# Fourteen attention pairs with both halves of the product with V in one step, on a fused attention and feed-forward kernel

## The chip, the cores and the metric

One NeuronCore of a Trainium2 chip runs the whole program. The metric is the device time of one execution in microseconds (us); the profiled execution is one more run, taken with the hardware profiler.

## The reference

Causal attention with a decay per position, then two feed-forward layers on its output:

```python
scores = scale * np.matmul(q, k.transpose(0, 1, 3, 2))      # (4, 8, 576, 576), head size 64
cum = np.cumsum(np.log(np.clip(f, 0.0001, 1.0)), axis=-1)
decay = cum[:, :, :, None] - cum[:, :, None, :]
scores = np.where(causal, -1000000000.0, scores + decay)
scores = scores - np.max(scores, axis=-1, keepdims=True)
attn = np.exp(scores)
attn = attn / (np.sum(attn, axis=-1, keepdims=True) + 1e-09)
x = np.matmul(attn, v)                                      # then (2304, 512)
h = x @ w_in;  y = (h * np.clip(h + 3.0, 0.0, 6.0) / 6.0) @ w_out
h = y @ w_in2; out = (np.maximum(h, 0.0) + alpha * np.minimum(h, 0.0)) @ w_out2
```

## The kernel before

The 32 heads are taken as 16 pairs (p = 0 to 15). A pair is nine units, and the attention loop makes one step for each unit: four of the first head (128 queries each, positions 0 to 3 of the pair), one joint unit for the last 64 queries of both heads (position 4), four of the second head (positions 5 to 8). A unit goes through the loop as a pipeline. At its own step TensorE makes its scores (`stage1`, L406 to L408, or L418 to L422 for the joint one); one step later VectorE takes the row maxima (`maxes`, L382); two steps later ScalarE takes the exponentials (`exps`, L389); five steps later TensorE transposes them (L437) and VectorE or ScalarE copies them out of PSUM (`evac`, L448, for the joint unit L452 and L455). The table `EV` says which engine copies: VectorE for the units with i = 3 (positions 3 and 8, 128x512), ScalarE for all others.

The scores lie in four PSUM banks that are used in turn. A unit takes the next bank, the joint one the next two, so a pair takes ten, and the scores at position n of a pair (0 to 3) go into the bank that position 5 + n of the pair before used. They wait until ScalarE has read it (`reader`).

The order within a step is written out by hand: transposes, maxima, exponentials, evacuations, work put down in `todo`, scores, and last the side work of `side`. Each engine takes its instructions in that order. The lists `CONV_ATT`, `CONV_ATT1` and `BUILD_ATT` give side work with its step: the unpacking of weights (m on ScalarE, L141; f and s on VectorE, L144 and L148; j, the join, L152; g, the sign, L157), their split into high and low parts (L195 on ScalarE, L199 on GpSimd), and the split of the attention output (L259 on ScalarE, L264 on GpSimd).

The product with V of pair p (`stage3`) falls into the steps of pair p + 1. It has two parts: queries 0 to 255 (part 0) and 256 to 575 (part 1). VectorE multiplies each part's result by the reciprocal sums (L502). In pairs 0, 1, 3 and 5 (`PIECE`) both parts are issued at position 7 of the next pair, part 0 into a PSUM buffer of the transposes (`pw`). In the other pairs part 0 is issued at position 6 and part 1 at position 8, and both use the one buffer `pv`, which the joint unit's `tq` (L441, position 0 of the pair after) uses too.

For the next heads, GpSimd scales and copies the query and the key (`prep_head`, L96) at positions 3 (`QA`) and 7 (`QB`) of each pair, GpSimd makes the key's low part (`low_k`, L370) and VectorE the query's (`low_q`, L375). The `low_q` of the head prepared at position 7 runs two steps later, at position 0 of the next pair, and the other at position 6.

After the attention the two feed-forward layers run on TensorE almost without a gap. At the very end `piece7` adds up partial products; for the text "23" it puts three operations at the front of the current step's list.

## Time and profile before

| | |
|---|---|
| median of 3 runs | 955.18 us (955.0 to 955.51) |
| the profiled execution's own time | 956.1 us |
| its span, first to last instruction | 953.9 us |
| mean granted TensorE clock | 0.998 |
| TensorE busy | 943.2 us, 99% |
| VectorE, ScalarE, GpSimd busy | 728.3, 552.6, 682.3 us |
| the chain that ended last | TensorE 91% of the span |

The time of an execution is a little longer than its span: 2.2 us lie around the span here. Busy TensorE time contains short waits inside of a run of matmuls, so the 99% don't say that nothing can be gained. The attention takes about the first 200 us, and there the start of one and the same instruction of each pair (the mask matmul of the joint unit, L422) shows how long a pair took.

### The profile page before, as it was taken

Reading aid. Unit: us, or ns where it says so; the run is one execution under the profiler, and the core shown is the slowest. Engines: PE = TensorE matmul, PEld = TensorE weight load, DVE = VectorE, ACT = ScalarE, POOL = GpSimd, SP = SyncE. Lnnn points to the kernel's source line nnn. Section 1 sums busy time; section 2 is a strip of 40 time slices with the busy share of each in tenths; the row PEclk is TensorE's granted clock in tenths of the full one; section 3 lists DMA queues with packets and bytes.
Section 4 is the critical chain, followed back from the end, with each engine's and each line's share of the span. In section 5 each row is a group of like instructions: output and inputs, shape, how many; then the busy total and the mean of one; then the engine's idle time right before and its main releaser. Section 6 shows DMA issues by size and latency. Waiting matters only on the chain.

```text
span 953.9 us, 16501 instructions
## 1 busy us (share of the span) xinstructions
PE 943.2 (99%) x5710; PEld 864.5 (91%) x5710; DVE 728.3 (76%) x1283; ACT 552.6 (58%) x1357; POOL 682.3 (72%) x670
## 2 busy tenths in 40 slices
PE   8999999999999999999999999999999999999998
PEld 5777777798999999999999999989899899899997
DVE  7899999857687877786788565357798778758787
ACT  6888887856654555464745366644445545464551
POOL 8678998666766466685766199666765678598886
PEclk9999999999999999999999999999999999999999
DMA  6766777301444344211587732414634420565641
GB/s 209 236 196 200 221 245 217 108 23 49 152 182 154 116 188 182 73 45 34 193 322 261 295 135 76 154 66 173 228 103 181 188 89 12 189 233 196 266 185 69
DMA packets 39511, 153.71 MB, mean 161 GB/s; under 512 B 5228, under 2 KB 5228, under 8 KB 36324
## 3 DMA queue, kind: packets, MB, share of 16 engines
q1 hardware_dynamic: 39424, 152.65, 45.2%
q8 instruction: 45, 0.74, 0.3%
q14 instruction: 38, 0.31, 0.1%
q10 hardware_dynamic: 4, 0.00, 0.0%
HBM read 101.40 MB, written 47.09 MB: 156 GB/s over the span
## 4 chain that ended last, share of the span: by engine, by line
PE 91%; DVE 4%; POOL 2%; ACT 1%; issue 1%; DMA 1%; POOLq 0%; DVEq 0%; ACTq 0%; SPq 0%
PE hA L812 20%; PE o L850 20%; PE o L852 15%; PE hC L812 10%; PE o L927 5%; PE hB L812 5%; PE tp L437 4%; PE pv L495 3%; PE sc L406 2%; PE sc L407 2%; PE sc L418 1%; PE sc L420 1%; PE sc L408 1%; PE tr L475 1%; POOL xl L264 1%
## 5 line engine op out<-in xcount | busy, mean ns | idle before, releaser
L758 POOL TENSOR_TENSOR g<-t,g 128x384 fp32r<-128x384 f32 x164 | 178.0, 1086 | 171.5 <-ACT g L757 164.8
L850 PE MATMUL o<-g,wo 128*128 128x384 f32 x1152 | 230.9, 339 | 1.2 <-POOL g L758 1.1
L812 PE MATMUL hA<-xh,wi 128*128 128x384 f32 x768 | 225.1, 337 | 0.6 <-ACT p L389 0.3
L850 PEld LDWEIGHTS o<-g,wo 128*128 128x128 f32 x1152 | 204.1, 188 | 2.4 <-POOL g L758 2.0
L757 ACT CAST g<-t 128x384 fp32r<-128x384 f32 x164 | 84.4, 514 | 145.9 <-DVE t L749 77.6
L852 PE MATMUL o<-wo,g 128*128 128x512 f32 x612 | 158.1, 394 | 0.0
L812 PEld LDWEIGHTS hA<-xh,wi 128*128 128x128 f32 x768 | 141.6, 188 | 3.3 <-DVE hD L826 0.6
L852 PEld LDWEIGHTS o<-wo,g 128*128 128x128 f32 x612 | 113.7, 188 | 18.7 <-POOL g L758 0.5
L812 PE MATMUL hA<-xl,wi 128*128 128x384 f32 x384 | 129.5, 337 | 0.0
L859 DVE SCALAR_TENSOR_TENSOR r<-o,r 128x384 f32<-128x384 f32 x168 | 92.3, 553 | 47.2 <-PE o L850 46.6
L812 PE MATMUL hC<-xh,wi 128*128 128x384 f32 x384 | 114.0, 337 | 0.0
L870 DVE TENSOR_TENSOR r<-o,r 128x512 f32<-128x512 f32 x90 | 61.6, 686 | 40.9 <-PE o L852 40.4
L389 ACT ACTIVATE p<-sc,nm 128x128 f32<-128x128 f32 (+2 forms) x144 | 80.3, 561 | 19.2 <-DVE nm L382 15.1
L382 DVE TENSOR_REDUCE nm<-sc 128x1 f32<-128x128 f32 (+2 forms) x144 | 71.6, 508 | 13.4 <-PE sc L408 8.3
L812 PEld LDWEIGHTS hA<-xl,wi 128*128 128x128 f32 x384 | 72.1, 188 | 2.3
L812 PEld LDWEIGHTS hC<-xh,wi 128*128 128x128 f32 x384 | 70.9, 188 | 1.5 <-issue 0.2
L264 POOL TENSOR_TENSOR xl<-r,xh 128x384 fp32r<-128x384 f32 x59 | 68.9, 1180 | 2.1 <-ACT xh L259 1.5
L437 PE MATMUL tp<-ident,p 128*128 128x128 f32 x384 | 66.7, 276 | 0.3 <-ACT pt L452 0.3
L817 ACT COPY s<-hA 128x384 f32<-128x384 f32 x96 | 45.9, 478 | 34.8 <-PE hA L812 34.4
L812 PE MATMUL hC<-xl,wi 128*128 128x384 f32 x192 | 64.8, 337 | 0.0
L812 PE MATMUL hB<-xh,wi 128*128 128x384 f32 x192 | 57.0, 338 | 0.0
L406 PE MATMUL sc<-k,q 128*128 128x256 f32 (+2 forms) x128 | 54.2, 424 | 0.9 <-DVE k L370 0.8
(209 smaller groups left out, 2056.7 us busy)
## 6 DMA issues: line engine op xcount, KB each, us to landing
wid<-wi SPq DMA_DIRECT2D x24, 896.0 KB
wi<-wid SPq DMA_DIRECT2D x12, 1792.0 KB
rqk<-in_qk SPq DMA_DIRECT2D x32, 608.0 KB
raw<-in_wi SPq DMA_DIRECT2D x32, 512.0 KB
raw<-in_wo SPq DMA_DIRECT2D x32, 512.0 KB
wod<-wo SPq DMA_DIRECT2D x24, 512.0 KB
wo<-wod SPq DMA_DIRECT2D x12, 1024.0 KB
vt<-in_v SPq DMA_DIRECT2D x16, 320.0 KB
```

The lines of the kernel that those rows point to most:

```text
L264: e.tensor_sub(out=XS[k][1][:, b, c], in0=x, in1=XS[k][0][:, b, c].bitcast(F32))
L382: last = waits("V", nc.vector.tensor_reduce(out=nm, in_=src, axis=AX.X if n == 1 else AX.XY, op=ALU.max, negate=True), last)
L389: last = waits("A", nc.scalar.activation(out=o, in_=src, func=AF.Exp, bias=nm, scale=1.0, accum_out=dst), last)
L406: waits("T", nc.tensor.matmul(out=sc[:, 0:n], lhsT=q1[:, qs], rhs=k1[:, 0:n], start=True, stop=False), *free)
L437: nc.tensor.transpose(tp[:, j, :], pt[:, 128 * j:128 * j + 128], ident)
L757: nc.scalar.copy(out=gt[n][i][:, 0], in_=hold["g"])
L758: nc.gpsimd.tensor_sub(out=gt[n][i][:, 1], in0=hold["g"], in1=gt[n][i][:, 0].bitcast(F32))
L812: nc.tensor.matmul(out=h, lhsT=a, rhs=b[:, x, kc], start=new and kc + e == 0, stop=kc == KH - 1 and e == 2, skip_group_check=not new)
L850: nc.tensor.matmul(out=o[:, 0:NB], lhsT=a[:, cs], rhs=b, start=st, stop=sp)
L852: nc.tensor.matmul(out=o, lhsT=b[:, cs], rhs=a, start=st, stop=sp)
L859: later(0, lambda: nc.vector.scalar_tensor_tensor(out=acc, in0=o[:, 0:NB], scalar=1.0 / 6.0, in1=acc, op0=ALU.mult, op1=ALU.add))
L870: nc.vector.tensor_add(out=acc, in0=o, in1=acc)
```

## The change

Four edits, all in the attention but the last:

- `PIECE` becomes all of 0 to 13, so the pairs 2, 4 and 6 to 13 take both parts of the product at position 7 of the next pair.
- In the lists of side work, the joins j of six weight quarters and the floors and shifts f, s of four go one step earlier. So the pairs with even p have their join at position 6 and their sign g behind the product at position 7; those with odd p have floor and shift at position 6.
- In the pairs of `EARLY` (3, 5, 7, 9, 11, 13), which are those in whose steps the product of an even pair falls (2, 4, ... 12), the 128x512 evacuation at position 8 goes from VectorE to ScalarE, and the `low_q` of the head prepared at position 7 is issued at position 8, at the front of the step's work, in place of position 0 of the next pair.
- At the end, the GpSimd addition of `kept["16"]` to `kept["23"]` is put at the end of the step's list in place of its front.

```diff
-    RD, SD, PM, PA, PB, PIECE = 3, 6, 8, 7, 9, (0, 1, 3, 5)
+    RD, SD, PM, PA, PB, PIECE = 3, 6, 8, 7, 9, range(14)
-    CONV_ATT = "m0 16 f0 24 s0 24 j0 34 g0 34 ... j1 52 g1 52 ... j2 70 g2 70 ... f3 79 s3 79 ... j3 88 g3 88 ..."
+    CONV_ATT = "m0 16 f0 24 s0 24 j0 33 g0 34 ... j1 51 g1 52 ... j2 69 g2 70 ... f3 78 s3 78 ... j3 87 g3 88 ..."
-    CONV_ATT1 = "... f0 97 s0 97 ... j0 106 g0 106 f1 115 s1 115 j1 124 g1 124 m2 125 f2 133 s2 133 ..."
+    CONV_ATT1 = "... f0 96 s0 96 ... j0 105 g0 106 f1 114 s1 114 j1 123 g1 124 m2 125 f2 132 s2 132 ..."
-    EV = (0, 0, 0, 1, 0, 0)
+    EV, EARLY = (0, 0, 0, 1, 0, 0), (3, 5, 7, 9, 11, 13)
...
-                rq, rk = raws.pop(h)
+                rq, rk = raws[h]
...
-                    copy = nc.vector.tensor_copy if EV[i] else nc.scalar.copy
+                    copy = nc.vector.tensor_copy if EV[i] and not (ab == 0 and p in EARLY) else nc.scalar.copy
...
-                        for fn, d in ((low_k, QL), (copy_k, QL), (low_q, QL if p else QL + 2)):
-                            todo.setdefault(t + d, []).append(lambda fn=fn, h=2 * p + 3: fn(h))
+                        for fn, d in ((low_k, QL), (copy_k, QL), (low_q, 1 if p in EARLY else QL if p else QL + 2)):
+                            todo.setdefault(t + d, []).insert(0 if d == 1 else 99, lambda fn=fn, h=2 * p + 3: fn(h))
...
-                flush, lambda: nc.vector.tensor_add(out=kept[2][0], in0=kept[2][0], in1=kept[1][0]),
-                lambda: nc.gpsimd.tensor_add(out=kept["23"], in0=kept["23"], in1=kept["16"])]
+                flush, lambda: nc.vector.tensor_add(out=kept[2][0], in0=kept[2][0], in1=kept[1][0])]
+            later(0, lambda: nc.gpsimd.tensor_add(out=kept["23"], in0=kept["23"], in1=kept["16"]))
```

How the instructions move, at the product of pair 2 (in the steps of pair 3), the first place of its kind. The list of each engine has one row for an instruction with its line, its output and inputs, and its size; "x2" is a count. On TensorE, from the transposes at position 7 on (`sc` scores, `tp` transposed probabilities, `pw` and `pv` the two parts of the product); the rows with + are new at that place, those with - were there before:

```order
 L437 MATMUL tp<-ident,p 128x128 x3
-L406 MATMUL sc<-k_760,q_758 128x384
-L407 MATMUL sc<-k_761,q_759 128x384
-L408 LDWEIGHTS identb
-L408 MATMUL sc<-maskb,identb 128x128
-L437 MATMUL tp<-ident,p 128x128 x4
+L495 MATMUL pw<-pt,vt 64x256 x2
+L495 MATMUL pw<-pt,vt 64x128 x2
 L495 MATMUL pv<-pt,vt 64x320 x6
 L495 MATMUL pv<-pt,vt 64x192 x2
 L495 MATMUL pv<-end_79,vt 64x64
 L495 MATMUL pv<-end_80,vt 64x64
```

The scores of position 7 and the four transposes of position 8 (`tp` x4), which stood ahead of part 1, now stand behind the whole product; part 0, which stood one step earlier, now stands right ahead of part 1.

On VectorE, from the query's low part at position 6 to the one after the product, before (`nm` are maxima, `wa` the weights in work, `r` the attention output, `pt` the copied transposes):

```order
L375 SCALAR_TENSOR_TENSOR q_847<-rqk,q_846 64x640
L502 TENSOR_TENSOR r_83<-pv,rcb 128x256
L382 TENSOR_REDUCE nm<-sc 128x1
L152 SCALAR_TENSOR_TENSOR wa<-raw,wa 128x512
L157 SCALAR_TENSOR_TENSOR wa<-raw,wa 128x512
L382 TENSOR_REDUCE nm<-sc 128x1
L448 COPY pt<-tp 128x4x128
L502 TENSOR_TENSOR r_83<-pv,rcb 128x320
L382 TENSOR_REDUCE nm<-sc 128x1
L375 SCALAR_TENSOR_TENSOR q_931<-rqk,q_930 64x640
```

and with the change:

```order
L375 SCALAR_TENSOR_TENSOR q_847<-rqk,q_846 64x640
L152 SCALAR_TENSOR_TENSOR wa<-raw,wa 128x512
L382 TENSOR_REDUCE nm<-sc 128x1
L502 TENSOR_TENSOR r_83<-pw,rcb 128x256
L502 TENSOR_TENSOR r_83<-pv,rcb 128x320
L157 SCALAR_TENSOR_TENSOR wa<-raw,wa 128x512
L382 TENSOR_REDUCE nm<-sc 128x1
L375 SCALAR_TENSOR_TENSOR q_944<-rqk,q_943 64x640
L382 TENSOR_REDUCE nm<-sc 128x1 x3
```

The sign (L157) now stands behind both multiplications, and the query's low part stands between the maxima of positions 7 and 8, where the copy stood.

On ScalarE, at position 8 of pair 3 (L389 with 128x256 are the exponentials of position 6; those of position 7, 128x384, follow the last row):

```order
 L448 COPY pt<-tp 128x3x128
 L389 ACTIVATE p,sm<-sc,nm 128x256
+L448 COPY pt<-tp 128x4x128
 L141 ACTIVATE wb<-raw 128x512
 L259 CAST xh_81<-r_83 128x384
```

The copy of the four transposes stands ahead of two pieces of side work and of the exponentials of position 7. GpSimd and the DMA queue keep their order in the attention; at the end of the program GpSimd takes one more product of the last layer (L758) ahead of its addition (L964).

## Rows read from the trace of the kernel before

**Rows 1.** The page, TensorE: busy us, share of the span, instructions.

```profile
PE 943.2 (99%) x5710; PEld 864.5 (91%) x5710; DVE 728.3 (76%) x1283; ACT 552.6 (58%) x1357; POOL 682.3 (72%) x670
```

**Rows 2.** Timeline of TensorE, L422 of pairs 2, 3, 5 to 7, 10 to 12, 15: start, us.

```profile
34.85 0.20 PE L422 MATMUL sc<-maskj,identb 128*128 128x64 bf16 x1
45.62 0.21 PE L422 MATMUL sc<-maskj,identb 128*128 128x64 bf16 x1
...
67.85 0.20 PE L422 MATMUL sc<-maskj,identb 128*128 128x64 bf16 x1
78.95 0.21 PE L422 MATMUL sc<-maskj,identb 128*128 128x64 bf16 x1
89.94 0.21 PE L422 MATMUL sc<-maskj,identb 128*128 128x64 bf16 x1
...
123.67 0.21 PE L422 MATMUL sc<-maskj,identb 128*128 128x64 bf16 x1
135.34 0.20 PE L422 MATMUL sc<-maskj,identb 128*128 128x64 bf16 x1
147.53 0.21 PE L422 MATMUL sc<-maskj,identb 128*128 128x64 bf16 x1
...
181.15 0.20 PE L422 MATMUL sc<-maskj,identb 128*128 128x64 bf16 x1
```

**Rows 3.** Waits of TensorE's weight loads for the product: us, times, longest.

```profile
PEld pv L495 <- issue: 3.8, 22, 0.2
```

**Rows 4.** Timeline of TensorE, two waits at the start of pairs 11 and 12.

```profile
131.60 0.36 PE L407 MATMUL sc<-k,q 68*128 68x256 f32 x1 [0.36 <-DMA k<-k]
143.35 0.27 PE L441 MATMUL tq<-ident,p 128*64 128x128 f32 x1 [0.64 <-DVE r L502]
```

**Rows 5.** Timeline, TensorE behind the product of pair 5.

```profile
83.83 0.44 PE L406 MATMUL sc<-k,q 128*128 128x384 f32 x1
...
84.35 0.60 PE L437 MATMUL tp<-ident,p 128*128 128x128 f32 x4
...
86.78 0.42 PE L406 MATMUL sc<-k,q 128*128 128x384 f32 x1
...
87.78 0.19 PEld L406 LDWEIGHTS sc<-k,q 128*128 128x128 f32 x1 [0.23 <-ACT p L389]
```

**Rows 6.** Timeline of ScalarE, at several places.

```profile
49.56 0.69 ACT L141 ACTIVATE wb<-raw 128x512 f32<-128x512 f32 x1
50.15 0.50 ACT L259 CAST xh<-r 128x384 fp32r<-128x384 f32 x1
...
85.65 0.58 ACT L389 ACTIVATE p<-sc,nm 128x384 f32<-128x384 f32 x1 [0.71 <-DVE nm L382]
...
86.94 0.70 ACT L389 ACTIVATE p<-sc,nm 128x512 f32<-128x512 f32 x1
...
90.77 0.59 ACT L476 COPY rcb<-tr 128x512 f32<-128x512 f32 x1
...
91.25 0.42 ACT L480 COPY rcb<-tj 64x64 f32<-64x64 f32 x2
```

**Rows 7.** Timeline of VectorE: pair 1's product, with TensorE's end; pair 2's sign.

```profile
39.51 0.28 PE L495 MATMUL pv<-end,vt 128*64 128x64 f32 x4
39.91 0.49 DVE L502 TENSOR_TENSOR r<-pv,rcb 128x320 f32<-128x320 f32 x1 [1.06 <-PE pv L495]
...
49.61 1.09 DVE L157 SCALAR_TENSOR_TENSOR wa<-raw,wa 128x512 uint32<-128x512 uint32 x1
50.62 0.55 DVE L382 TENSOR_REDUCE nm<-sc 128x1 f32<-128x384 f32 x1
```

**Rows 8.** One line's instructions, L375: ns min/median/max.

```profile
L375 DVE SCALAR_TENSOR_TENSOR q<-rqk,q x32: 802/1032/2058, 8.4 to 177.5; 64x640 fp32r<-64x640 f32 x32
```

**Rows 9.** Timeline of GpSimd beside the sign of rows 7.

```profile
49.00 1.16 POOL L96 TENSOR_SCALAR q<-rqk 128x640 fp32r<-128x640 f32 x1
```

**Rows 10.** Timeline of the weight loads at the program's end.

```profile
946.46 2.85 PEld L852 LDWEIGHTS o<-wo,g 128*128 128x128 f32 x13 [0.47 <-POOL g L758]
```

More of the change, by code (lines that the diff above doesn't have):

```diff
@@ L43, in decay_attention_ffn2_kernel @@
     LM, LE, LT, LV = 1, 2, 5, 5
-    RD, SD, PM, PA, PB, PIECE = 3, 6, 8, 7, 9, (0, 1, 3, 5)
+    RD, SD, PM, PA, PB, PIECE = 3, 6, 8, 7, 9, range(14)
     DRAIN = {9 * NP + 3: 2, 9 * NP + 4: 2, 9 * NP + 6: 2, 9 * NP + 7: 2}
-    CONV_ATT = "m0 16 f0 24 s0 24 j0 34 g0 34 r0 38 m1 35 f1 42 s1 42 j1 52 g1 52 m2 53 r1 56 S1 57 S3 58 S2 60 f2 60 s2 60 ha 61 hb 61 la 67 lb 68 S4 70 j2 70 g2 70 hc 71 m3 71 r2 75 lc 77 f3 79 s3 79 hd 80 ho0 80 wi0 84 ld 86 lo0 88 j3 88 g3 88 wi1 92 r3 93 ho1 98 lo1 103 wo0 104 wo1 113"
-    CONV_ATT1 = "r0 110 r1 126 m0 89 f0 97 s0 97 m1 98 j0 106 g0 106 f1 115 s1 115 j1 124 g1 124 m2 125 f2 133 s2 133 S1 133 j2 142 g2 142 S3 142 S2 143 ha 146 hc 146 hb 147 la 147 lc 147 lb 148 S4 149 hd 149 ld 150 m3 150 f3 151 s3 151 j3 152 g3 153"
+    CONV_ATT = "m0 16 f0 24 s0 24 j0 33 g0 34 r0 38 m1 35 f1 42 s1 42 j1 51 g1 52 m2 53 r1 56 S1 57 S3 58 S2 60 f2 60 s2 60 ha 61 hb 61 la 67 lb 68 S4 70 j2 69 g2 70 hc 71 m3 71 r2 75 lc 77 f3 78 s3 78 hd 80 ho0 80 wi0 84 ld 86 lo0 88 j3 87 g3 88 wi1 92 r3 93 ho1 98 lo1 103 wo0 104 wo1 113"
+    CONV_ATT1 = "r0 110 r1 126 m0 89 f0 96 s0 96 m1 98 j0 105 g0 106 f1 114 s1 114 j1 123 g1 124 m2 125 f2 132 s2 132 S1 133 j2 142 g2 142 S3 142 S2 143 ha 146 hc 146 hb 147 la 147 lc 147 lb 148 S4 149 hd 149 ld 150 m3 150 f3 151 s3 151 j3 152 g3 153"
     BUILD_ATT = "h00 25 l00 32 h01 35 l01 40 h10 43 l10 50 h11 53 l11 79 a30 79 h20 80 a31 88 h21 89 l20 95 a40 97 l21 97 h30 98 l30 104 a41 106 h31 107 h40 107 l31 113 l40 115 a60 115 h41 116 l41 122 a61 124 a50 124 h60 125 a51 130 l60 131 h61 134 h50 134 h51 134 l61 139 l50 140 l51 142"
```

## The prediction

> **What bounds the kernel now.** I read the page first, then TensorE's waits, then the timeline of the attention engine by engine. The page shows TensorE busy for 99% of the span [rows 1], so only work taken from TensorE's own stream, or waits inside it, can move the time. In the attention I take L422, which comes once in each pair, as a clock [rows 2]. The L422 of pairs n and n + 1 enclose the product of pair n - 1. From 67.85 to 78.95 lies the split product of pair 4: 11.10 us. From 34.85 to 45.62 lies the product of pair 1, already in one piece: 10.77 us. So one piece is worth 0.33 us in a pair that waits for nothing. About half of that is one start of the product less: 22 starts of `pv` lost 3.8 us, 0.17 us each [rows 3].
>
> Not every one-piece pair gets it. Pair 5, in one piece, took 10.99 (78.95 to 89.94), and pair 3 took 11.13 (45.62 to 67.85 is 22.23 for pairs 2 and 3, less 11.10 for pair 2, which is split like pair 4). Behind the product of pair 5 the scores of position 3 waited for the exponentials of position 8, four units earlier, to free their bank [rows 5]. So the bound of a one-piece pair is the chain behind the product: transposes or maxima, exponentials of positions 7 and 8, bank. The split pairs have waits of their own further on: `tq` waited 0.64 us for VectorE to empty `pv`, which part 1 had filled only one step earlier, and a score waited 0.36 us for the copy of the key [rows 4]. That is why pairs 9 and 10 took 11.67 and 12.19 (123.67 to 135.34 to 147.53).
>
> **The change, part by part.** Ten pairs change: even ones 2, 4, 6, 8, 10, 12 and odd ones 7, 9, 11, 13. Before, they took 11.10 each (2 and 4), 33.73 together (6, 7, 8), 11.67 (9), 12.19 (10) and 33.62 together (11, 12, 13) [rows 2].
>
> *Odd pairs.* Their floors and shifts go one step ahead, which is the layout that pairs 1, 3 and 5 have already, and nothing goes to ScalarE. Their waits there were 0, 0.36 and 0.22 (from 10.77). In pairs 3 and 5 VectorE came late to the product, in pair 1 it didn't; I take 10.77 for pairs 7, 11 and 13, with 11.13 as the upper bound. For pair 9 I leave half of its excess over 11.10, since the copy of the key is a transfer that the change doesn't touch: 10.77 + 0.28 = 11.05.
>
> *Even pairs, ScalarE.* Here the copy of the four transposes goes to ScalarE, and it stands ahead of two side operations and of the exponentials of position 7. Count from T, the start of the scores of position 7, the first instruction behind the product (83.83 in pair 5). The four transposes end at 84.35 + 0.60, that is T + 1.12 [rows 5]. A ScalarE copy of 128x512 holds the next instruction back by 0.48 (90.77 to 91.25), the unpacking by 0.59 (49.56 to 50.15), and the 0.50 us cast by about 0.40, as its neighbours' bars overlap by 0.10 [rows 6]. So the exponentials of position 7 start at T + 2.59; in pair 5 they started at T + 1.82. Those of position 8 follow 1.29 later (85.65 to 86.94), with the copies of the joint unit between them: T + 3.88. They last 0.70, and the scores of position 3 started 0.14 after their end (87.64 to 87.78) [rows 5, 6]: T + 4.72. In pair 5 these scores came at T + 3.95 after a wait of 0.23, so unhindered at T + 3.72. The wait is 1.0 us. Before, the two side operations lay under the product, with ScalarE idle before the exponentials; that cover is gone, because the copy ahead of them can't start until the product is through.
>
> *Even pairs, VectorE.* The multiplication of part 1 starts 0.12 after TensorE's last product (39.79 to 39.91) [rows 7], about T + 0.2. The sign follows 0.41 later and holds the maxima of position 7 back by 1.01 (49.61 to 50.62) [rows 7]: T + 1.62. After 0.47 (its 0.55 less the same overlap) comes the query's low part, 0.80 at least and 1.03 in the median [rows 8], then the maxima of position 8 at T + 2.8 to T + 3.05. In pair 5 the exponentials of position 8 came 0.89 after their maxima, here at T + 3.7 to T + 3.95. So VectorE is late by as much as ScalarE, and taking the copy off VectorE gains little, since the query's low part fills its place. The join one step ahead costs nothing as long as VectorE is done with it when the product ends, which the product covers. I add 0.1 us on average for even pairs in which the sign or the low part meets GpSimd: wait 1.1, pair 11.87. For pair 10, whose VectorE was late anyway, I take 12.1.
>
> *What the even pairs lose.* Queued behind the waiting scores is the whole rest of TensorE's stream, so the wait comes in full.
>
> *Sum.* Pairs 2 and 4: 2 x (11.87 - 11.10) = +1.5. Pairs 6 to 8: 11.87 + 10.77 + 11.87 - 33.73 = +0.8. Pair 9: 11.05 - 11.67 = -0.6. Pair 10: 12.1 - 12.19 = -0.1. Pairs 11 to 13: 10.77 + 11.87 + 10.77 - 33.62 = -0.2. Together +1.4 us. So a one-piece product gains 0.33 us per pair and frees `tq`, and the chain behind it takes a little more back.
>
> *The end.* GpSimd makes the low part of the last product ahead of its addition. A weight load waited 0.47 us for it, mostly under running matmuls [rows 10]; the gain is 0 to 0.47, and I take 0.1, near the lower end, as TensorE itself shows no gap there. The addition comes about as much later, ahead of GpSimd's last additions, whose sum of work stays the same.
>
> Work behind the attention keeps its order, and TensorE hardly waits there [rows 1], so I let the +1.4 come through: +1.3 with the end. The profiled execution, 956.1 us, would give 957.4; the median of the runs shown lies 0.9 below it, so I forecast 955.18 + 1.3 = **956.5 us**. A change of less than 0.2%, 1.9 us, can't be told from none, so the forecast itself is "within".
>
> **The rivals.**
>
> *A. The chain behind the product hides, and the merge pays.* If the even pairs wait no more than pairs 3 and 5 do, 0.29 us on average, they take 11.06. Then pairs 2 and 4 give -0.1, 6 to 8 give 32.89 - 33.73 = -0.8, 9 gives -0.6, 10 gives -1.1, 11 to 13 give 32.60 - 33.62 = -1.0, the end -0.1: -3.7, **951.5 us**. With no wait at all the ten pairs would take 107.7 in place of 113.4: -5.7, 949.5 us. For it speaks that pair 1 is clean and that both late chains are estimates of a few tenths. Against it, ScalarE takes in program order, and the transposes it has to copy stand behind the product. It decides below 0.6 us of wait per even pair, where the sum falls under -1.9.
>
> *B. GpSimd and VectorE meet in the even pairs, and the time rises.* Place: the sign and the query's low part, which now both stand between the product and the maxima of position 8. The low part took up to 2.06 us [rows 8]. At that length the maxima of position 8 come at 1.62 + 0.47 + 1.98 = T + 4.07, the exponentials at T + 4.96 and the scores at T + 5.80: a wait of 2.1 us, 1.0 more than forecast. One such pair gives +2.3 us, which is just slower; three give +4.3, **959.5 us**; all six +7.3, 962.5. For it: the sign of pair 2 ran from 49.61 to 50.70 beside a GpSimd instruction from 49.00 to 50.16 [rows 7, 9], and GpSimd is busy for 72% of the span [rows 1]. Against: such long ones are few, since the median is 1.03. The Trainium skill, "SBUF — State Buffer", in its section on the two sides of SBUF, says that a VectorE instruction with two SBUF inputs and a GpSimd instruction exclude each other for a whole instruction, and don't share. By that rule the sign of pair 2 could begin its work only at 50.16; the trace agrees so far as it ends 0.54 later, and the rule would make rival B the rule rather than the exception for pairs in which GpSimd has no gap.
>
> *C. Nothing of it shows.* The waits may trade places with those that the key's copy or GpSimd cause in pairs 6 to 10 anyway; then the ten pairs keep their 113.4 us and the time stays at **955.2 us**. It is part of "within".
>
> **How the numbers follow.** A forecast within 1.9 us, with C: 0.44. A, faster: 0.20, as two engines would both have to be earlier than their rows say. B or a wait of more than 1.2 us on ScalarE alone, slower: 0.36; it is the larger of the two, as the forecast lies on its side and 0.6 us more are enough. The range leaves out the clean case of A and the far half of B: 952.8 to 959.7 us.
>
> **What would show it.** In the changed profile the L422 of the pairs 7 to 8, 9 to 10, 11 to 12 and 13 to 14 become about 11.9 apart (the even products 6, 8, 10, 12), and 8 to 9, 12 to 13, 14 to 15 about 10.8; the waits of `tq` for L502 go. Even pairs show weight loads of L406 waiting for L389 by about a microsecond, with ScalarE's copy, unpacking, cast and exponentials back to back ahead of it. Even pairs at 11.1 or less make the forecast wrong by A. Sums of L422 that differ from the change of the whole time would show that the feed-forward part moved, which I count at nothing.

## The result, and the profile after

| | before | with the change |
|---|---|---|
| median, runs side by side | 955.64 us (955.0 to 956.65, 6 runs) | 960.6 us (960.14 to 961.89, 6 runs) |
| ratio | | 1.0053, interval 1.0042 to 1.0064 |
| the profiled execution's own time, span | 956.1, 953.9 us | 961.89, 960.1 us |
| mean granted TensorE clock | 0.998 | 0.998 |

The change makes the kernel 5.0 us slower. The forecast was 956.5 us with a range up to 959.7: the sign was that of the forecast, the size was not, and the time lies above the range. The profiled execution is often one of the slower ones of its kernel (961.89 us here, with a median of 960.6), so pairs are read from the profiles and times from the medians.

The page of the changed kernel, busy time by engine, answers to [rows 1]:

```profile
PE 943.8 (98%) x5710; PEld 865.3 (90%) x5710; DVE 732.3 (76%) x1277; ACT 555.1 (58%) x1363; POOL 680.7 (71%) x670
```

The busy time of every engine is within 4 us of before, so the 5 us are waits. VectorE's 4.0 us more are no more work either: six of its copies (0.68 us each) went to ScalarE, and its bars contain the waits for GpSimd that are described below. L422 in TensorE's timeline (start, us), with which the prediction measured the pairs, answers to [rows 2]; these are pairs 2 to 4, 8, 9 and 12 to 14:

```profile
35.51 0.20 PE L422 MATMUL sc<-maskj,identb 128*128 128x64 bf16 x1
46.27 0.21 PE L422 MATMUL sc<-maskj,identb 128*128 128x64 bf16 x1
58.41 0.20 PE L422 MATMUL sc<-maskj,identb 128*128 128x64 bf16 x1
...
104.70 0.20 PE L422 MATMUL sc<-maskj,identb 128*128 128x64 bf16 x1
116.34 0.20 PE L422 MATMUL sc<-maskj,identb 128*128 128x64 bf16 x1
...
151.89 0.20 PE L422 MATMUL sc<-maskj,identb 128*128 128x64 bf16 x1
162.65 0.21 PE L422 MATMUL sc<-maskj,identb 128*128 128x64 bf16 x1
174.93 0.20 PE L422 MATMUL sc<-maskj,identb 128*128 128x64 bf16 x1
```

46.27 to 58.41 is the product of pair 2: 12.14 us, where 11.87 was forecast and 11.10 stood before. 104.70 to 116.34 is that of pair 7: 11.64, forecast 10.77. 151.89 to 162.65 is pair 11 at 10.76, the forecast to a hundredth. All pairs, in us, with three runs from below (the two columns on the right leave out the key's low part; the numbers are differences of L422 starts):

| product of pair | forecast | before | change | change, cover and sign moved | change, no key low | cover, sign, no key low |
|---|---|---|---|---|---|---|
| 2 | 11.87 | 11.10 | 12.14 | 11.06 | 11.82 | 10.83 |
| 4 | 11.87 | 11.10 | 12.25 | 10.84 | 11.84 | 10.84 |
| 6 | 11.87 | 11.50 | 11.94 | 11.32 | 11.95 | 10.84 |
| 8 | 11.87 | 11.11 | 12.41 | 11.00 | 11.81 | 10.82 |
| 10 | 12.1 | 12.19 | 11.77 | 10.82 | 11.66 | 10.83 |
| 12 | 11.87 | 11.10 | 12.28 | 12.45 | 11.83 | 10.84 |
| 7 | 10.77 | 11.12 | 11.64 | 12.27 | 10.79 | 10.76 |
| 9 | 11.05 | 11.67 | 11.37 | 11.63 | 11.34 | 10.76 |
| 11 | 10.77 | 11.28 | 10.76 | 12.79 | 10.76 | 10.76 |
| 13 | 10.77 | 11.24 | 11.92 | 11.58 | 11.06 | 10.81 |
| sum | 114.8 | 113.4 | 118.5 | 115.8 | 114.9 | 108.1 |

The ten pairs took 5.1 us more than before, 3.7 more than forecast: 1.3 in the even pairs, 2.3 in the odd ones. The spans of the two profiles differ by 6.2 us. The rest lies outside these pairs: from the last L422 to the end of the span are 773.2 us, 772.8 before, and the L422 of pair 2 came 0.66 us later (35.51, before 34.85), ahead of anything the change touches. That start scatters between runs: the first L422 lies between 14.0 and 15.5 us. In both of these profiles TensorE's granted clock is 0.50 of full speed, 1.2 GHz, for some 3 us ahead of it (11 to 14 us); in others it is 1.00 there.

The waits of TensorE between 25 and 188 us (what it waited for: us in all, times, longest), after:

```profile
PEld sc L406 <- ACT p L389: 9.9, 18, 0.9
```

and the same view of before:

```profile
PEld sc L406 <- ACT p L389: 0.6, 2, 0.3
```

Scores wait for a bank, that is for exponentials, as forecast. No wait of a score for the key or for GpSimd is left in that view. But what holds the exponentials? Pair 2's product, all engines (start, us, instruction; in brackets what ended the idle time before it):

```profile
48.23 1.47 POOL L264 TENSOR_TENSOR xl<-r,xh 128x384 fp32r<-128x384 f32 x1
48.76 1.48 DVE L152 SCALAR_TENSOR_TENSOR wa<-raw,wa 128x512 uint32<-128x512 uint32 x1
...
51.14 0.44 PE L406 MATMUL sc<-k,q 128*128 128x384 f32 x1
51.33 0.49 DVE L502 TENSOR_TENSOR r<-pv,rcb 128x320 f32<-128x320 f32 x1 [0.42 <-ACT p L389]
51.55 1.41 POOL L370 TENSOR_TENSOR k<-rqk,k 64x576 fp32r<-64x576 f32 x1
51.74 1.77 DVE L157 SCALAR_TENSOR_TENSOR wa<-raw,wa 128x512 uint32<-128x512 uint32 x1
52.31 0.59 ACT L448 COPY pt<-tp 128x512 f32<-128x512 f32 x1 [1.07 <-PE tp L437]
52.79 0.70 ACT L141 ACTIVATE wb<-raw 128x512 f32<-128x512 f32 x1
53.37 0.52 ACT L259 CAST xh<-r 128x384 fp32r<-128x384 f32 x1
53.43 0.55 DVE L382 TENSOR_REDUCE nm<-sc 128x1 f32<-128x384 f32 x1
53.90 0.81 DVE L375 SCALAR_TENSOR_TENSOR q<-rqk,q 64x640 fp32r<-64x640 f32 x1
54.08 0.58 ACT L389 ACTIVATE p<-sc,nm 128x384 f32<-128x384 f32 x1 [0.18 <-DVE nm L382]
...
55.40 0.69 ACT L389 ACTIVATE p<-sc,nm 128x512 f32<-128x512 f32 x1
...
56.23 0.19 PEld L406 LDWEIGHTS sc<-k,q 128*128 128x128 f32 x1 [0.58 <-ACT p L389]
```

T is 51.14. ScalarE runs as forecast: copy at T + 1.17 (forecast 1.12), unpacking, cast, done with them at T + 2.75. VectorE does not. The sign takes 1.77 us, because GpSimd began the key's low part 0.19 us before it, and the maxima of position 7 start at T + 2.29, forecast T + 1.62. So the exponentials wait for the maxima (0.18 us in brackets), start at T + 2.94 instead of T + 2.59, and the scores of position 3 come at T + 5.09 instead of T + 4.72. The join at 48.76 is as long, and costs nothing here: it lies under the product.

In an odd pair, the product of pair 7 (its T is 109.56):

```profile
106.64 1.74 POOL L199 TENSOR_TENSOR wi<-wc,wi 128x512 fp32r<-128x512 f32 x1
107.17 1.50 DVE L144 TENSOR_SCALAR wa<-wa 128x512 f32<-128x512 f32 x1
...
109.95 0.48 ACT L389 ACTIVATE p<-sc,nm 128x256 f32<-128x256 f32 x1 [1.68 <-DVE nm L382]
...
111.24 0.51 ACT L259 CAST xh<-r 128x384 fp32r<-128x384 f32 x1
...
111.65 0.58 ACT L389 ACTIVATE p<-sc,nm 128x384 f32<-128x384 f32 x1
...
112.08 1.41 POOL L370 TENSOR_TENSOR k<-rqk,k 64x576 fp32r<-64x576 f32 x1
112.24 1.93 DVE L375 SCALAR_TENSOR_TENSOR q<-rqk,q 64x640 fp32r<-64x640 f32 x1
...
113.79 0.19 PEld L406 LDWEIGHTS sc<-k,q 128*128 128x128 f32 x1 [0.48 <-ACT p L389]
114.09 0.60 DVE L382 TENSOR_REDUCE nm<-sc 128x1 f32<-128x128 f32 x2
114.46 0.37 ACT L389 ACTIVATE p<-sc,nm 128x128 f32<-128x128 f32 x1 [0.58 <-DVE nm L382]
```

Two things hold this pair. The floor takes 1.50 us, the shift behind it 0.83, and the maxima of position 6 come late: ScalarE waits 1.68 us for them and starts the exponentials of position 6 at T + 0.39. Its side work of this place, two pieces of weights' high parts (L195) and the cast (L259), then lies behind the product and not under it, and the exponentials of position 7 follow the cast without a wait at T + 2.09; the scores of position 3 come at T + 4.23. Later the query's low part, here still at position 0 of the next pair, runs beside the key's low part and holds the maxima of the next pair's first unit back to 114.09.

Pair 11 (T is 156.76) took 10.76 us, although its floor took 1.22 us too:

```profile
157.04 0.50 ACT L259 CAST xh<-r 128x384 fp32r<-128x384 f32 x1
...
158.17 0.58 ACT L389 ACTIVATE p<-sc,nm 128x384 f32<-128x384 f32 x1 [0.63 <-PE sc L406]
```

ScalarE has one cast there and not three pieces of side work, and its exponentials of position 7, at T + 1.41, wait for nothing but the scores themselves; the scores of position 3 come at T + 3.73. Pairs 9 and 13 have three pieces of side work like pair 7. So the scores of position 3 are 0.50, 0.45 and 1.16 us late in pairs 7, 9 and 13, which took 0.88, 0.61 and 1.16 us over 10.76. Late maxima of position 6 and ScalarE's own side work come together in them; no run moved that side work of the odd pairs alone.

### The profile page after: what moved, and what is told of

The parts are those of the page before. It is cut to its first block, busy times and chain, and to the rows that moved or that the text cites. A ratio compares the mean times of both kernels' runs of the same rounds, so it can differ in the third digit from the quotient of the medians.

```text
span 960.1 us, 16508 instructions
## 1 busy us (share of the span) xinstructions
PE 943.8 (98%) x5710; PEld 865.3 (90%) x5710; DVE 732.3 (76%) x1277; ACT 555.1 (58%) x1363; POOL 680.7 (71%) x670
## 4 chain that ended last, share of the span: by engine, by line
PE 90%; DVE 4%; ACT 2%; issue 2%; POOL 2%; DMA 1%; ACTq 0%; DVEq 0%; POOLq 0%
PE hA L812 20%; PE o L850 20%; PE o L852 15%; PE hC L812 10%; PE o L927 5%; PE hB L812 5%; PE pv L495 3%; PE tp L437 3%; PE sc L406 2%; PE sc L407 2%; PE pw L495 1%; DVE nm L382 1%; PE sc L418 1%; PE sc L420 1%; ACT p L389 1%
## 5 line engine op out<-in xcount | busy, mean ns | idle before, releaser
L758 POOL TENSOR_TENSOR g<-t,g 128x384 fp32r<-128x384 f32 x164 | 177.8, 1085 | 171.8 <-ACT g L757 165.1
L389 ACT ACTIVATE p<-sc,nm 128x128 f32<-128x128 f32 (+2 forms) x144 | 80.4, 563 | 25.7 <-DVE nm L382 22.1
L382 DVE TENSOR_REDUCE nm<-sc 128x1 f32<-128x128 f32 (+2 forms) x144 | 70.9, 506 | 11.4 <-PE sc L408 6.1
```

The lines of the kernel that those rows point to most:

```text
L382: last = waits("V", nc.vector.tensor_reduce(out=nm, in_=src, axis=AX.X if n == 1 else AX.XY, op=ALU.max, negate=True), last)
L389: last = waits("A", nc.scalar.activation(out=o, in_=src, func=AF.Exp, bias=nm, scale=1.0, accum_out=dst), last)
L758: nc.gpsimd.tensor_sub(out=gt[n][i][:, 1], in0=hold["g"], in1=gt[n][i][:, 0].bitcast(F32))
```

## What a meeting of VectorE and GpSimd is, read from the trace

For every VectorE instruction of five kinds between 25 and 191 us of the changed kernel that began while a GpSimd instruction ran, I took its end less the end of that GpSimd instruction, and its duration where no GpSimd instruction was beside it (anywhere in the trace):

| VectorE instruction | alone, us | met | ends after GpSimd's end by, us |
|---|---|---|---|
| query's low part L375, 64x640 | 0.81 | 23 | 0.67 to 0.72, one 0.80 |
| join L152, 128x512 | 0.68 | 7 | 0.54 to 0.55 |
| sign L157, 128x512 | 0.68 | 6 | 0.54 to 0.55 |
| floor L144, 128x512 | 0.41 | 6 | 0.27 to 0.28 |
| shift L148, 128x512 | 0.43 | 6 | 0.28 to 0.29 |

In 46 of the 48 the VectorE instruction ends its own lone time, less 0.13 or so, after GpSimd's, whichever GpSimd instruction it was; the other two, 0.72 and 0.80, met less than its last 0.1 us. It does not share; it waits the other out in full. The sign above: GpSimd's ends at 51.55 + 1.41 = 52.96, the sign at 51.74 + 1.77 = 53.51, 0.55 later. GpSimd's next instruction waits out VectorE's in the same way: in pair 11 the key's low part, 1.41 us alone, began at 159.40 beside the query's, which ended at 160.00, and ended 1.29 us after it. The maxima (L382, 128x384), which read PSUM, keep their 0.50 to 0.56 us, though GpSimd ran beside 26 of 28. In the kernel before, 44 meetings show the same numbers, but for two that met less than GpSimd's last 0.01 us. The Trainium skill says this in "SBUF — State Buffer", section "Who interferes with whom": the pair of SBUF ports that the two engines share is locked for a whole instruction, between a GpSimd instruction that reads SBUF and VectorE operations with two SBUF inputs or, with a single one, in a two-port mode. The trace agrees, with the numbers of the table, for the query's low part, join and sign; all GpSimd instructions that they met read SBUF. The floor and the shift, with one SBUF input each, wait in the same way; in which mode they run no row shows. I had left them out when I cited the rule.

What changed is how much is waited out. Over its lone time an instruction took, between 25 and 188 us: a join 0.23 us more before and 0.89 after, a floor 0.39 and 0.75, a sign 0.43 and 0.81, a query's low part 0.33 and 0.37, but a shift 0.41 and 0.34; in all 19.5 us before and 28.3 after. The order of the prediction's section on the change lets one see why. Before, a multiplication and maxima (PSUM readers) stood between the query's low part and the join, and GpSimd's held-back instruction ran under them. Now the join follows directly (47.73 + 1.10 is 48.83, the join began at 48.76): as the low part lets go, GpSimd's waiting instruction starts, and the join waits that out too. The floor follows the low part in the same way in odd pairs. That the order is the reason is my reading of these rows; no run changed it alone.

## The experiments

"Cover" is ScalarE's side work of position 8, "sign" the signs of the even pairs.

**Which chain holds the even pairs.** Cover: the unpacking (five pieces, not the four of the expected text) and high parts one step earlier, under the product. Sign: the signs two steps later, behind both maxima. Then both.

```diff
 cover
-m1 35 m2 53 m3 71 hc 71 | m0 89 m2 125 | h01 35 h11 53 h21 89 h31 107 h40 107 h60 125
+m1 34 m2 52 m3 70 hc 70 | m0 88 m2 124 | h01 34 h11 52 h21 88 h31 106 h40 106 h60 124
 sign
-g0 34 g1 52 g2 70 g3 88 | g0 106 g1 124 r1 126
+g0 36 g1 54 g2 72 g3 90 | g0 108 g1 126 r1 127
```

> The change, with ScalarE's side work of position 8 in the steps of the even products (four unpackings, six casts of the attention output, one cast of weights) one step earlier, so that it lies under the product and not behind the copy. Theory S (ScalarE's queue behind the copy is what the even pairs wait for): the exponentials of position 7 start near T + 1.7 in place of T + 2.9, the even pairs fall from 12.1 on average to about 11.3, the time by some 5 us, to 956. Theory V (VectorE's maxima come late, since the sign ahead of them meets GpSimd): those exponentials still wait for maxima at T + 2.3, even pairs stay at 12.0 or more, the time falls by less than 1 us.

Cover alone: 960.4 us, ratio 1.005 (1.0035 to 1.0065). Pairs 2, 4 and 8 stay at 12.15, 12.23 and 12.38. The rows of VectorE and ScalarE at pair 2 show why:

```profile
51.07 1.77 DVE L157 SCALAR_TENSOR_TENSOR wa<-raw,wa 128x512 uint32<-128x512 uint32 x1
52.77 0.54 DVE L382 TENSOR_REDUCE nm<-sc 128x1 f32<-128x384 f32 x1
...
53.41 0.58 ACT L389 ACTIVATE p<-sc,nm 128x384 f32<-128x384 f32 x1 [1.18 <-DVE nm L382]
```

ScalarE is free and waits 1.18 us for maxima behind the 1.77 us sign. But pairs 6, 10 and 12 fall to 11.53, 11.55 and 11.47 (11.94, 11.77 and 12.28 with the change). In pairs 6 and 10 of the changed kernel the maxima of position 7 came at T + 1.68 and T + 1.58, about as forecast, and ScalarE's side work held the exponentials to T + 2.77 and T + 2.48. So theory V holds for three even pairs, theory S for two of the others; the median moved by 0.2 us.

> The change, with the sign of the six even pairs two steps later, behind the maxima of position 8 in place of ahead of those of position 7. Theory V: maxima of position 7 at about T + 0.8 in place of T + 2.3, and ScalarE's queue becomes the bound at T + 2.6 for the exponentials of position 7, so each even pair gains 0.3 to 0.4 and the time falls by about 2 us, to 958.5. Theory S: the same bound was there before, so nothing is gained (under 0.5 us). If a sign placed there delays the next pair's first maxima, the time rises.

Sign alone: 959.26 us, 1.0036 (1.0023 to 1.005). The same place:

```profile
51.17 0.56 DVE L382 TENSOR_REDUCE nm<-sc 128x1 f32<-128x384 f32 x1
...
53.47 0.67 DVE L157 SCALAR_TENSOR_TENSOR wa<-raw,wa 128x512 uint32<-128x512 uint32 x1
...
52.68 0.50 ACT L259 CAST xh<-r 128x384 fp32r<-128x384 f32 x1
...
53.08 0.58 ACT L389 ACTIVATE p<-sc,nm 128x384 f32<-128x384 f32 x1
```

The maxima are early, the sign is short, and the exponentials follow ScalarE's own cast without a wait. Pairs 2, 4, 8 and 12 fall to 11.81 to 11.96: that is ScalarE's chain, forecast as 11.87. With VectorE's chain they took 0.32 to 0.45 us more. Pairs 6 and 10 keep their 11.93 and 11.78.

> Both edits together. If the two chains lie side by side, each hiding the other, as I now think, only this one helps in full: exponentials of position 7 near T + 1.7, of position 8 near T + 3.0, a wait of about 0.1 to 0.3 in the even pairs, 10.9 to 11.1 each, the time 6 to 7 us under the change: 953.5 to 954.5, faster than before. Theory S alone gives the time of the run with the side work moved, theory V alone that of the run with the sign moved.

Both: 958.17 us, 1.0025 (1.0015 to 1.0034). Even pairs 2, 4, 8 and 10 fall to 10.82 to 11.06 as expected, pair 6 to 11.32: neither engine holds them alone. But pair 3 went from 11.13 to 11.99, pair 7 from 11.64 to 12.27, pair 11 from 10.76 to 12.79, pair 12 stays at 12.45, and the time missed the expected one by 4 us. At pair 11 TensorE and GpSimd show a new wait:

```profile
159.47 0.40 PE L418 MATMUL sc<-k,q 128*128 128x288 f32 x1 [1.71 <-POOL k L370]
```

```profile
154.08 0.73 POOL L96 TENSOR_SCALAR q<-rqk 128x640 fp32r<-128x640 f32 x1 [2.51 <-DMA rqk<-in_qk]
```

Pair 12 is long for another reason, TensorE's granted clock. It was 1.00 until that wait. Behind it, two rows of busy times (PE, PEld, DVE, ACT, POOL, then PEclk, DMA share, GB/s) show:

```profile
161.00:162.00 1.00, 1.00 (x8) 0.91 (x7) 0.45 (x2) 0.82 (x4) 0.92 (x2) 0.57 0.31 109
162.00:163.00 1.00, 1.00 (x7) 0.91 (x6) 1.00 (x2) 0.98 (x4) 0.95 (x1) 0.50 0.46 97
```

PEclk 0.50 is 1.2 GHz, half of full speed. The clock is back at 1.00 from 165 us on. Without the key's low part (below), where TensorE has no such wait, it stays at 1.00 and pair 12 takes 10.84.

**Are the odd pairs long by themselves?** The kernel before, with the odd pairs alone in one piece, and the end's edit.

```diff
-PIECE = range(14)      EARLY = (3, 5, 7, 9, 11, 13)      j0 33 ... j1 123
+PIECE = (0, 1, 3, 5, 7, 9, 11, 13)      EARLY = ()      j0 34 ... j1 124
```

> The kernel before with the odd pairs 7, 9, 11, 13 alone in one piece, floors and shifts one step earlier, and the end's addition moved; the even pairs as before. The forecast for these four pairs was 43.4 us in place of 45.3; in the changed kernel they took 45.7. Theory P (their waits there come from the phase in which the even pairs leave VectorE and GpSimd): here they take about 43.5 and the time is 953.7. Theory O (it is the layout's own: floor, shift and the query's low part meet GpSimd wherever they are): they take 45 or more, and the time stays at 955.6.

956.04 us, 1.0009 (1.0 to 1.0018). Pairs 7, 9, 11 and 13 take 46.87 us together, 45.31 before: they lose by their own layout, with the even pairs left alone. That sum is of the profiled execution, the slowest of ten (957.93 us); by the medians the layout costs 0.6 us, where a gain of 1.9 was expected.

**Does the copy belong on ScalarE?**

```diff
-copy = nc.vector.tensor_copy if EV[i] and not (ab == 0 and p in EARLY) else nc.scalar.copy
+copy = nc.vector.tensor_copy if EV[i] else nc.scalar.copy
```

> The change, with the copy at position 8 of the even products back on VectorE; everything else as changed. If the copy on ScalarE is what the even pairs wait for (theory S), ScalarE's side work lies under the product again and the even pairs fall to about 11.3, the time to 956. If the chain on VectorE is the bound (sign, maxima, query's low part, maxima), the copy adds its 0.6 us to it ahead of the maxima of position 8: even pairs about 12.6 on average in place of 12.1, the time 3 to 4 us more, 964.

967.7 us, 1.0132 (1.0116 to 1.0148), 3.7 more than expected, pair 8 at 15.35 and pair 12 at 14.19. On VectorE the copy stands behind the sign and ahead of the query's low part and the maxima of position 8; it is late itself and makes them later (waits of weight loads, 25 to 188 us):

```profile
PEld sc L406 <- ACT p L389: 11.3, 10, 2.4
...
PEld tp L437 <- DVE pt L448: 2.2, 4, 0.8
```

In pairs 8 and 12 the low part, moved back, also meets the whole of the key's (2.05 and 2.04 us), TensorE stands still for 2.2 us ahead of the scores of position 3, and with or behind each of these two waits TensorE's granted clock is at 0.50 again (128 to 131.5 us and 179.3 to 182.7), which the expected time didn't contain. So of the change's parts the copy on ScalarE is a help, given the rest.

**Without the key's low part.** GpSimd's low part of the key is left out from the fifth head on (its place keeps the copy of the key), in the changed kernel, in the one with cover and sign moved, and in the kernel before. That takes away GpSimd's most frequent part in these meetings (20 of the 48), and some 42 us of its work. Between 25 and 188 us of the changed kernel 33 of 47 meetings stay, and what they add to the lone times falls from 28.3 to 13.7 us.

```diff
+                if h >= 4:
+                    return
                 low.tensor_sub(out=k1[64:128], in0=rk[64:128], in1=k1[64:128].bitcast(F32))
```

> The change without GpSimd's low part of the key from head 4 on (L370, 28 instructions); the key's low rows then hold the high part, so the scores differ from the reference. If VectorE's side work is long because it meets GpSimd's instructions, signs fall from 1.0 to 1.9 us to 0.7 to 1.1, joins too, the odd pairs fall from 11.4 to about 10.8 and the even ones by the 0.3 us that VectorE is behind ScalarE: 956. If the meetings don't matter, the pairs keep their lengths and the time stays within 1 us of 960.6.

956.53 us, 1.001 (1.0001 to 1.002). Pair 2 again (lines are 2 higher here):

```profile
51.16 0.44 PE L408 MATMUL sc<-k,q 128*128 128x384 f32 x1
...
51.76 0.68 DVE L157 SCALAR_TENSOR_TENSOR wa<-raw,wa 128x512 uint32<-128x512 uint32 x1
52.36 0.55 DVE L384 TENSOR_REDUCE nm<-sc 128x1 f32<-128x384 f32 x1
...
53.81 0.57 ACT L391 ACTIVATE p<-sc,nm 128x384 f32<-128x384 f32 x1
55.10 0.69 ACT L391 ACTIVATE p<-sc,nm 128x512 f32<-128x512 f32 x1
...
55.93 0.19 PEld L408 LDWEIGHTS sc<-k,q 128*128 128x128 f32 x1 [0.58 <-ACT p L391]
```

Sign 0.68 us, maxima at T + 1.20, exponentials at T + 2.65 and T + 3.94, scores at T + 4.77: the forecast's ScalarE chain (2.59, 3.88, 4.72) to 0.06 us. Five of the even pairs take 11.81 to 11.95, pairs 7 and 11 take 10.79 and 10.76. Pair 9 keeps 11.34 with short low parts: there ScalarE's side work still lies behind the product. The ten pairs sum to 114.9 us, forecast 114.8, with the even ones 0.5 less and the odd ones 0.6 more.

> The same left out of the run with both ScalarE's side work and the sign moved (958.2). If meetings of VectorE and GpSimd make up what is left there, all pairs fall to 10.8 to 10.9 and the time to about 950. If the inputs come late (GpSimd waited 2.0 us for the load of a query and key in pair 4 of that run), the odd pairs stay above 11.3 and the time at 955 or more.

949.95 us, 0.9945 (0.993 to 0.9959): every pair at 10.76 to 10.84.

> The kernel before without GpSimd's low part of the key (L370) from the fifth head on; the low part of those keys is left out. Control for the run of the changed layout without it (949.95 us, all pairs at 10.76 to 10.83). Theory G (the merge is worth what was forecast for it, 0.33 us in each of ten pairs and some waits of tq, and only the meetings of VectorE and GpSimd take it back): split pairs here at 11.0 to 11.1, so ten times 0.3 more, 953.0 to 953.8 us. Rival N (the merge is worth nothing by itself, and the leave-out alone brings the time down): 950 us, pairs at 10.8.

The control, 953.09 us, 0.9975 (0.9966 to 0.9985): split pairs at 11.11 to 11.13. So without this partner the one-piece layout is worth 3.1 us if cover and sign are moved as well (949.95 against 953.09), and costs 3.4 as the change has it (956.53). With it the same two differences are +2.7 (958.17 against 955.46) and +5.0. The ten pairs of the control take 111.2 us, so the key's low part costs 2.2 us in the ten pairs of the kernel before (113.4) and 3.6 in those of the changed one (118.5 against 114.9). The forecast set out from pairs that contain those 2.2 us and ended, at 114.8, on the sum of a kernel without the key's low part: that is 3.6 of the 3.7 us by which its ten pairs were too short. The leave-out alone can't tell the meetings from the rest of what that instruction costs.

**Even pairs alone, with cover and sign moved.** PIECE without 7, 9, 11 and 13, their floors and shifts back.

> Only the even pairs 2, 4, ... 12 in one piece, with the copy on ScalarE, the side work moved and the sign behind the maxima of position 8; pairs 7, 9, 11, 13 split as before. The even pairs took 10.8 to 11.3 in the run with both edits, where the odd ones in one piece grew. If the odd pairs' growth came from their own layout, they stay at 11.1 to 11.7 here and the six even pairs give 2 to 3 us: 952.5 to 953.5, faster than before. If every us won by the even pairs comes back as a wait for inputs or GpSimd in the odd ones, the time stays at 955 to 956.

956.34 us, 1.0014 (1.0004 to 1.0023), a miss by 3 us, and just above the second expectation: the even pairs stay low (10.86 to 11.56), but pairs 3 and 11 are long here too, 11.68 and 12.57.

**Are the loads late behind a queued fetch?** In these kernels the later sign also frees the raw weights later, and the next fetch of weights stands ahead of query and key in the queue. Six fetches were moved three steps later.

> The third run's kernel (cover and sign moved, 958.17 us), with the six fetches of raw weights that are issued in the steps after a sign two or three steps later, so that the loads of query and key don't stand behind a fetch that still waits for the sign. Theory Q (the later sign held the queue, and through it GpSimd's copies and the key's low part): waits of L96 for its load in pairs 3 and 11 go, pair 3 back to 11.1 or 11.3 (from 11.99), pair 11 to 11.6 or less (from 12.79), time 956 us. Rival G (only the meetings of VectorE and GpSimd lengthen those pairs): 958 us as before, odd pairs as they were.

959.15 us, 1.0044 (1.0029 to 1.0059), above either expectation. Pair 3 falls to 10.78, as that theory says, but pair 11 rises to 13.06: there the score now waits for the copy of the key, a transfer.

```profile
159.67 0.37 PE L420 MATMUL sc<-k,q 68*128 68x288 f32 x1 [1.97 <-DMA k<-k]
```

Pair 12 follows at 12.73, with the clock at 0.50 from 161 to 164.5 us as in the third run. So the queue explains pair 3, and not pair 11.

**The query's low part in its old place,** in the changed kernel and with cover and sign moved.

```diff
-(low_q, 1 if p in EARLY else QL if p else QL + 2)
+(low_q, QL if p else QL + 2)
```

> The changed kernel with the query's low part back in its old place (position 0 of the next pair), the copy of position 8 still on ScalarE. Theory G: behind the product VectorE then has multiplication, sign and the two maxima only, so the maxima of position 8 come about 1 us earlier; ScalarE's copy, unpacking and cast still hold the exponentials, so even pairs fall by 0.3 us or so, to 11.9, but the low part then stands ahead of the maxima of the next pair's first units, where the odd pairs pay: 959 to 962 us in all. Rival (the low part in the place of the copy costs nothing where it is, and VectorE has no other gap for it): 964 us or more, as in the run with the copy back on VectorE (967.7).

> The third run's kernel (cover and sign moved, 958.17 us) with the query's low part back at position 0 of the next pair as well. Theory G: behind the product neither engine has side work now, so even pairs stay at 10.9 to 11.1; the low part then meets GpSimd elsewhere, and the odd pairs decide: 956 to 959 us. Rival Q (the queue of loads decides the odd pairs in the third run): the same odd pairs as there, 958 us.

960.83 us, 1.0059 (1.0042 to 1.0076), and 961.39 us, 1.0062 (1.0047 to 1.0077). In the first the even pairs 2 to 8 hardly move (12.10, 12.23, 11.90, 12.34): the low part's place is not what held them, and the expected 0.3 us did not come; only pair 12 fell, to 11.80. The second was expected lower by both theories; its pairs 2 and 4 are at 10.8, and from pair 6 on all are between 11.66 and 12.46.

**The same work on VectorE.** The leave-out removes meetings, work and any lateness of GpSimd together. Here nothing is left out: VectorE makes the key's low part, for all heads from the fifth on, for the even ones, for the odd ones, and for all on the kernel before (the first three with cover and sign moved).

```diff
-low = nc.vector if h < 2 and LS0[h] == "V" else nc.gpsimd
+low = nc.vector if (h < 2 and LS0[h] == "V") or h >= 4 else nc.gpsimd
```

> The third run's kernel (cover and sign moved, 958.17 us) with the key's low part (L370) on VectorE in place of GpSimd for all heads from the fifth on. Nothing is left out, so this separates the meetings from the work. An instruction of this kind took 0.76 us on VectorE in the prologue, 28 of them are 21 us. Theory G (a meeting costs VectorE as much as it would cost to do the work itself): the query's low parts fall from 1.19 to 0.86 us and the joins and floors shorten, VectorE's bars come to some 156 us of the 163 between 25 and 188 us, and the pairs mostly keep 10.8 to 11.1: 951 to 954 us. Rival W (VectorE has no room for 21 us more, wherever it stands): 958 us or more, with waits for the maxima in all pairs.

> As the run with the key's low part on VectorE, but for the even heads alone (prepared at position 3, two steps before their low parts); the odd heads' stays on GpSimd. Theory G: half of the way from 958.2 to 950 and VectorE 10 us busier, 953 to 956 us, with long query's low parts left for the odd heads alone. Rival W: 958 us.

> As the run before, but for the odd heads alone (prepared at position 7, key's low part at position 0 of the next pair). Theory G: 953 to 956 us; better than the even heads' if the meetings that count are those just behind the product. Rival W: 958 us or more, as the instruction then stands ahead of the maxima of the next pair's first unit.

> The kernel before with the key's low part on VectorE for all heads from the fifth on; the layout is not changed. Control for the first of these runs. Theory G: between the kernel before and its run without that low part (953.09 us), 953.5 to 955.5. Rival W: 957 us or more.

962.72 (1.0068, 1.0051 to 1.0085), 958.2 (1.0022, 1.0013 to 1.0031), 961.5 (1.0052, 1.0037 to 1.0066) and 966.46 us (1.0105, 1.009 to 1.012): rival W, in all four. Busy times from 25 to 188 us in the first (PE, PEld, DVE, ACT, POOL, then PEclk, DMA share, GB/s):

```profile
25.00:188.00 163.00, 159.71 (x1274) 119.88 (x1272) 156.46 (x308) 132.73 (x468) 87.84 (x100) 1.00 0.67 202
```

VectorE is at 156.5 us of 163. The query's low parts did fall to 0.90 us, but the 28 new instructions took 1.00 us each instead of the 0.76 that I reckoned with, since twelve of them met what is left on GpSimd (0.87 to 1.62 us; the others 0.76). What the five kinds of the table waited out fell from 26.6 us in the third run to 8.8, and the kernel still lost 4.5 us: where VectorE has no room, the meetings cost less than the work that makes them.

**The parts that stood best.** One piece in pairs 0 to 6, 8 and 10 only, cover and sign moved for those, key's low part on VectorE for even heads 4 to 14; and the same with it left on GpSimd.

> A try at a kernel that beats both: one piece only in the even pairs 2 to 10 (split as before in 7, 9 and 11 to 13), with the cover and sign moved for those pairs, and the key's low part on VectorE for the even heads up to 14. Summed from the pairs of the runs in which each part stood best (pairs 2 to 5 as with the key's low part on VectorE for even heads, 10.77 to 10.96; 6 to 10 as with even pairs alone, 55.5 together; 11 to 13 as before, or 1.3 more if the wait that pair 10 loses comes back in pair 11): 953 to 954.5 us against 955.5 before. Rival: waits move rather than vanish, because VectorE's 147 to 158 us of bars in 163 us bound the sum of the pairs: 955.5 to 957.

> The same with the key's low part left on GpSimd. It tells what that part of the first is worth: by the pairs of the earlier runs 0.3 to 1 us more than the first, 954 to 955.5 us. Rival as there: 955.5 to 957 us, and no difference between the two.

The first takes 954.1 us against 955.5, ratio 0.9985 (0.9976 to 0.9994), the second 956.13, 1.0008 (0.9999 to 1.0017). The first is as expected and beats the kernel before by 1.4 us; the second is 0.6 above its expected range. Of the fifteen kernels here, the changed one among them, that leave nothing out and have more pairs in one piece than before, the first is the only one under before, so its 0.15% is the best of fifteen tries. Pairs 2 to 5 keep their 10.75 to 10.97, but pair 11 rises to 12.45 again: part of the wait only moves.

## Why the prediction was wrong

- **One piece is worth 0.33 us a pair: right.** Without the key's low part split pairs take 11.11 to 11.13 and one-piece pairs, with cover and sign moved as well, 10.76 to 10.84.
- **Even pairs, ScalarE's chain: right,** in pair 2 to 0.06 us at each of its steps, as the run without the key's low part shows, and in place in the changed kernel, where it is the bound of pairs 6 and 10. The cover under the product is gone, as the text had it.
- **Even pairs, VectorE "late by as much as ScalarE", and "0.1 us on average" for GpSimd: this term failed.** The sign was priced from [rows 7] at the 1.01 us that it held the maxima back in pair 2, where it met GpSimd's last 0.55 us of a copy. In the changed order the signs took 1.04 to 1.88 us, two of them beside nearly a whole key's low part. Alone, VectorE's maxima come at T + 1.20 and would let the exponentials start some 0.8 us before ScalarE is ready for them; with the meeting they start 0.2 us after it (T + 2.94 against T + 2.75). That was so in pairs 2 and 4; in pairs 8 and 12 the query's low part was long as well (1.16 us), and the maxima of position 8 came at T + 3.63 and T + 3.62. The even pairs took 1.3 us more in all than forecast.
- **"I take 10.77 for pairs 7, 11 and 13": this step failed,** and it was the larger one: 11.64, 10.76, 11.92, with 11.37 for pair 9. I had priced them by pair 1, the one pair of this layout whose floor met nothing (0.41 us at 37.32 in the trace of before), and taken 11.13 from pairs 3 and 5 as the upper bound. Pairs 1, 3 and 5 also have no side work of ScalarE between the exponentials of positions 6 and 7; pairs 7, 9 and 13 have three pieces, which I counted in the even pairs and put at nothing in the odd ones. Low part, floor and shift, long beside GpSimd, made the maxima of position 6 late; that brought this side work out from under the product, at up to 1.16 us a pair. A long floor alone cost pair 11 nothing. The run with the odd pairs alone shows that the loss is their layout's own. Without the key's low part pair 7 falls to 10.79 and pair 13 to 11.06, and pair 9 stays at 11.34. That ScalarE's side work is the other half is read from the rows of these pairs.
- **Rival B, the meetings: its mechanism, not its place.** It had three or six even pairs with a long low part or sign. The trace has all six even signs met, at a smaller price each, and more of it in odd pairs, where no rival looked. That the rule of the lock made B the rule was said in the prediction, and then hardly taken into the sum (0.1 us for an even pair) or the chances. Rivals A and C are out.
- **The end: nothing, near the 0.1 forecast.** The weight load's wait of [rows 10] is gone and the time behind the attention did not fall (773.2 us, 772.8 before).
- **Left open:** the 1 to 2 us of pair 11 in the runs with early even pairs. In three of them TensorE waited for the key's low part behind a load that came 2.0 to 2.5 us late for GpSimd, in one for the key's copy; no run told which comes first.

## What to carry to other kernels

Where VectorE and GpSimd both work from SBUF to SBUF, price each VectorE instruction at its lone time plus the rest of whatever GpSimd instruction runs when it begins, and see which one that will be in the new order; a median of the old order is no price. Readers of PSUM between two such VectorE instructions seem to give GpSimd its turn at no cost, by the rows read here; no run tried that alone. Price a pair by all pairs of its layout, not by the clean one, and with the side work of its own steps. Behind a long wait of TensorE look at its granted clock too.

## What the runs showed of the hardware

- The meetings are exact: 48 of 48 VectorE instructions ended 0.27 to 0.80 us after the GpSimd instruction that they met, by kind to within 0.02 us but for two low parts that met its very end, and instructions with a single SBUF input (0.41 us alone, up to 1.63) wait as those with two.
- Taking 42 us of work from GpSimd, which no TensorE instruction of the changed kernel's attention was seen waiting for, made that kernel 4.1 us faster (960.6 to 956.53), the one with cover and sign moved 8.2 us (958.17 to 949.95), and the kernel before 2.4 us (955.47 to 953.09).
- In four places of three runs TensorE stood still for 1.7 to 2.2 us in the attention, and with or behind each of these waits its granted clock fell from 1.00 to 0.50 (1.2 GHz) and was back at 1.00 some 3.4 us later; pair 12 behind such a place took 12.45 us, and 10.84 in the run without the wait and without the fall.
